# Scaling the first MLP's normalized tiles on ScalarE, and W1's splits put behind the first product

## The chip, the cores and the metric

The kernel runs on one core of a Trainium2 chip. A core has engines that each work through a queue of their own in order: TensorE (PE, with PEld for its weight loads), VectorE (DVE), ScalarE (ACT), GpSimd (POOL), and SyncE (SP), which issues most transfers. The metric is the device time of one execution in microseconds, lower is better.

## What is computed

The reference does three things in a row for 8 batches of 512 rows with 8 heads, and 32 state rows per batch. Attention runs both ways between the rows and the state. Its output, 4608 rows of 512 values, goes through a first MLP with a softmax gate and a normalization, and then through a second MLP with a sigmoid gate:

```python
# attention, both ways, concatenated to 4608 x 512
h = x @ w_in                                   # 512 -> 1024
sm = softmax(h)
solu = h * sm
mu = mean(solu); var = mean((solu - mu) ** 2)
ln = (solu - mu) / sqrt(var + 1e-06) * g_ln
x = ln @ w_out                                 # 1024 -> 512
h = x @ w_in2                                  # 512 -> 2048
out = (h * sigmoid(1.702 * h)) @ w_out2        # 2048 -> 512
```

Inputs are doubles; each is turned into 32-bit floats on the chip. A product with full accuracy is made of three matmuls: every factor is split into a high part, which is a cast, and a low part, which is a subtraction (`split` does this for weights, `mm3` is the three matmuls: high by high, high by low, low by high; in the profile lines 422, 423 and 424).

## The kernel before

The kernel doesn't issue instructions as it is written. Each step is recorded by `do(engines, function, reads, writes, key, after)`, with one or more engines that could do it and an assumed cost for each. `plan()` then puts the steps of all engines in an order, from the assumed costs and due times, chooses the engine where there is a choice, and gives each tile its buffer. `emit()` writes the instructions in that order. So a change of one step's engine, cost or predecessors shifts the choices for many other steps. `after=` names further steps that must be planned before this one; it stands for order only, no data goes between them.

The first MLP works on tiles of 128 rows: 4 tiles for each of the 8 batches, and 2 for the state rows, 34 in all. For one tile, `mlp1(b, i, key)` records:

- PE: the product that gives h (12 matmuls: two groups of heads, two halves of 512 columns, three each; 24 for the tiles of the state rows),
- DVE: the row maximum (L771); ACT: the exponential u, with its row sum (L773); DVE: u = h times u, with its row sum (L775),
- ACT: one value per row for the small term of the variance (L779); DVE: minus the mean into column 3 of the small tile `s` (L780),
- ACT: the sum of (u - mean) squared (L781); DVE: the variance into column 6 (L783),
- POOL: column 6 to the power -0.5 into column 7 (L785), one value per row,
- DVE or POOL: u = (u + column 3) * column 7 over 128x1024 values (L786), in place.

What follows reads u: `z_T` transposes four tiles' blocks of 128 columns on PE (L827), ACT makes the high part while it scales by g (L833), DVE the low part (L835), and `mlp1_out` multiplies by W2. From batch 3 to 7 one half of the columns goes through `z_turn` instead, which transposes on DVE (L797) and with transfers. The gated tile in PSUM takes a pair of banks; at most three such pairs are in use at once.

W1 is used in two ways. For batches 0 and 1 it is multiplied unsplit by the state rows' transposes (`state_w1`, L671). From batch 2 on, products with split W1 are used (`state_w1_both`), and the eight splits (4 blocks of rows by 2 halves of the columns; `hi_w1s` is a cast on ACT or DVE, `lo_w1s` a subtraction on POOL or DVE, L458) are recorded in the main loop with batch 1, before batch 1's attention. Their due times come from `W1S`; nothing else holds them back.

The second MLP (from about 420 us on) has its weights prepared earlier, between the batches.

## Time and profile before

| | us |
| --- | --- |
| median of 3 runs | 1127.77 (1125.75 to 1128.52) |
| profiled execution | 1126.07 |
| its span in the profile | 1124.3 |
| PE busy | 1080.0 (96%) |
| DVE busy | 825.2 (73%) |
| ACT busy | 637.8 (57%) |
| POOL busy | 258.7 (23%) |

The shares are averages over the whole span. To read what paces the kernel, one looks at busy times stretch by stretch, since the attention and first MLP (up to some 350 us) and the second MLP have different limits. Then the waits of PE name who released it, and the timeline shows what stood in that engine's queue. Mean durations hide that one and the same operation may take very different times when another engine works beside it; the timeline shows single ones.

### The profile page before, as it was taken

The page shows a single profiled execution, that of the slowest core. Times are in us where ns is not written, and L with a number is a line of the kernel's source. Part 1 is how long each engine was busy: PE and PEld are TensorE (multiplying, and loading weights), DVE is VectorE, ACT ScalarE, POOL GpSimd, SP SyncE. Part 2 cuts the span into 40 slices and gives each one's busy share as a digit, 9 for nine tenths or more (in the row PEclk, how much of TensorE's full clock was granted, in tenths as well). Part 3 has the DMA queues.
Part 4 walks back from the last instruction along what each step waited for, and adds up shares of the span by engine and source line. Part 5 has one row for each costly group of instructions (what it writes and reads, how often), then busy time and mean ns, then how long its engine had stood idle before and what let it go on. Part 6 is the DMA issues. An engine that isn't in the chain of part 4 may idle for free.

```text
span 1124.3 us, 21689 instructions
## 1 busy us (share of the span) xinstructions
PE 1080.0 (96%) x8055; PEld 976.9 (87%) x8055; DVE 825.2 (73%) x1398; ACT 637.8 (57%) x1171; POOL 258.7 (23%) x218
## 2 busy tenths in 40 slices
PE   6798999799899999999999999999999999999998
PEld 2466677577677889999999999999999999999998
DVE  6999878988989746628757755634388888788874
ACT  6686756866868546547666656545244444344341
POOL 3865443743746701301111000000000000000000
PEclk8899999999999999999999999999999999999999
DMA  8214234568673569998667657559944254344431
GB/s 242 67 39 113 78 70 135 165 126 177 187 162 87 158 153 365 334 374 276 230 233 242 237 204 257 179 209 398 383 145 125 64 170 150 101 144 151 134 93 57
DMA packets 233082, 202.78 MB, mean 180 GB/s; under 512 B 128784, under 2 KB 174864, under 8 KB 232976
## 3 DMA queue, kind: packets, MB, share of 16 engines
q1 hardware_dynamic: 232880, 201.26, 57.3%
q8 instruction: 63, 1.03, 0.4%
q14 instruction: 43, 0.35, 0.1%
q10 hardware_dynamic: 96, 0.13, 0.1%
HBM read 113.25 MB, written 82.84 MB: 174 GB/s over the span
## 4 chain that ended last, share of the span: by engine, by line
PE 75%; DVE 13%; issue 3%; SPq 3%; POOL 3%; DMA 2%; ACT 1%; DVEq 0%; POOLq 0%; ACTq 0%
PE psum L1098 9%; PE psum L1100 9%; PE psum L1099 9%; PE psum L1010 9%; PE psum L1011 9%; PE psum L1012 9%; PE psum L422 5%; PE psum L423 5%; PE psum L424 4%; DVE w_w L449 1%; DVE w_w L444 1%; SPq L529 1%; POOL lo_w3s L458 1%; DVE w_w L447 1%; DVE u L775 1%
## 5 line engine op out<-in xcount | busy, mean ns | idle before, releaser
L1098 PE MATMUL psum<-w4r,hi_g 128*128 128x256 f32 x896 | 251.8, 281 | 1.6 <-DVE oc L1109 1.6
L1100 PE MATMUL psum<-w4r,lo_g 128*128 128x256 f32 x896 | 251.6, 281 | 0.0
L1099 PE MATMUL psum<-w4r,hi_g 128*128 128x256 f32 x896 | 251.6, 281 | 0.0
L1098 PEld LDWEIGHTS psum<-w4r,hi_g 128*128 128x128 f32 x896 | 169.1, 189 | 1.8 <-ACT hi_g L463 1.8
L1100 PEld LDWEIGHTS psum<-w4r,lo_g 128*128 128x128 f32 x896 | 169.3, 189 | 0.0
L1099 PEld LDWEIGHTS psum<-w4r,hi_g 128*128 128x128 f32 x896 | 169.0, 189 | 0.0
L463 ACT CAST hi_g<-a_g 128x512 fp32r<-128x512 f32 x124 | 75.4, 620 | 127.3 <-DVE a_g L880 87.1
L451 POOL TENSOR_TENSOR w_w<-w_w,raw_w 128x512 uint32<-128x512 uint32 x48 | 68.9, 1441 | 284.1 <-DVE w_w L449 206.1
L1022 DVE TENSOR_TENSOR c<-psum,u 128x512 f32<-128x512 f32 x64 | 44.1, 689 | 98.0 <-PE psum L1012 63.7
L422 PE MATMUL psum<-zhi,hi_w 128*128 128x512 f32 (+1 forms) x288 | 113.9, 395 | 1.3 <-DVE zlo L835 0.6
L424 PE MATMUL psum<-zhi,lo_w 128*128 128x512 f32 (+1 forms) x288 | 109.9, 382 | 0.0
L957 DVE TENSOR_TENSOR lo_g<-a_g,hi_g 128x512 fp32r<-128x512 f32 x128 | 84.0, 685 | 19.9 <-PE psum L1099 7.1
L994 ACT ACTIVATE t<-c 128x512 f32<-128x512 f32 x96 | 60.5, 632 | 50.0 <-DVE c L1022 49.9
L957 DVE TENSOR_TENSOR lo_g<-gr,hi_g 128x512 fp32r<-128x512 f32 x104 | 71.0, 685 | 11.8 <-ACT hi_g L463 9.2
L423 PE MATMUL psum<-zlo,hi_w 128*128 128x512 f32 (+1 forms) x208 | 78.3, 376 | 0.2
L463 ACT CAST hi_g<-gr 128x512 fp32r<-128x512 f32 x104 | 61.8, 618 | 28.4 <-PE psum L1099 14.4
L422 PEld LDWEIGHTS psum<-zhi,hi_w 128*128 128x128 f32 x288 | 54.2, 188 | 17.3 <-issue 4.1
L424 PEld LDWEIGHTS psum<-zhi,lo_w 128*128 128x128 f32 x288 | 54.1, 188 | 11.8 <-DVE lo_w L458 0.4
L1010 PE MATMUL psum<-hi_x,w3r_1h 128*128 128x256 f32 x224 | 63.1, 282 | 1.2 <-ACT u L1017 1.2
L1011 PE MATMUL psum<-lo_x,w3r_2h 128*128 128x256 f32 x224 | 63.1, 282 | 0.0
L1010 PE MATMUL psum<-hi_x,w3r_2h 128*128 128x256 f32 x224 | 63.0, 281 | 0.0
L1011 PE MATMUL psum<-lo_x,w3r_3h 128*128 128x256 f32 x224 | 63.0, 281 | 0.0
(261 smaller groups left out, 3101.9 us busy)
## 6 DMA issues: line engine op xcount, KB each, us to landing
g<-t SPq DMA_DIRECT2D x136, 256.0 KB, 3.4
gr<-g SPq DMA_DIRECT2D x136, 256.0 KB, 3.4
w4r<-w4k SPq DMA_DIRECT2D x56, 256.0 KB, 5.2
raw_w<-in_moe_w_in SPq DMA_DIRECT2D x24, 512.0 KB, 6.0
raw_w<-in_moe_w_out SPq DMA_DIRECT2D x24, 512.0 KB, 4.2
xb<-scr SPq DMA_DIRECT2D x34, 256.0 KB, 6.3
scr<-x SPq DMA_DIRECT2D x16, 512.0 KB, 3.6
out<-oc SPq DMA_DIRECT2D x32, 256.0 KB, 3.8
```

What stands on the lines that cost most here:

```text
L422: nc.tensor.matmul(o, lhi, rhi, start=first, stop=False)
L423: nc.tensor.matmul(o, lhi, rlo, start=False, stop=False)
L424: nc.tensor.matmul(o, llo, rhi, start=False, stop=last)
L451: do(POOL(1.23), lambda e: e.tensor_tensor(u(), u(), raw()[:, :, 0], op=ALU.add), [w, raw], [w], key=due)
L463: e.copy(o, i)
L957: do(DVE(.68), lambda e: e.tensor_tensor(flat_(lo), flat_(t), flat_(hi), op=ALU.subtract), [t, hi], [lo], key=due)
L1010: nc.tensor.matmul(o, wh()[:, k, cut], hi()[:, k, :], start=first and not mi + k, stop=False, **OPEN)
L1011: nc.tensor.matmul(o, wh()[:, k, cut], lo()[:, k, :], start=False, stop=False, **OPEN)
L1012: nc.tensor.matmul(o, wl()[:, k, cut], hi()[:, k, :], start=False, stop=bool(mi and k), **OPEN)
L1098: nc.tensor.matmul(o, hi()[:, mi, cut], wt[:, 0], start=first, stop=False, **OPEN)
L1099: nc.tensor.matmul(o, hi()[:, mi, cut], wt[:, 1], start=False, stop=False, **OPEN)
L1100: nc.tensor.matmul(o, lo()[:, mi, cut], wt[:, 0], start=False, stop=2 * j + mi == NM - 1 and u == 1, **OPEN)
```

## The change

The scaling of the normalized tile is written as u = u * r + m * r with r the power -0.5 of the variance and m minus the mean, and is done by ACT in place of DVE or POOL. For that, POOL's step computes two columns: r in column 7 (as before; line 786 of the new kernel) and m * r in column 8 (line 787). Its assumed cost goes from .46 to .92; the ACT step (line 790) is assumed at 1.1. It applies to all 34 tiles.

`split` gets a parameter `after`, given to the cast. The eight W1 splits pass `after=[first0]`, where `first0` is the last product step of batch 0's first tile, `mlp1(0, 0)`. Everything else is as it was; lines after the first MLP are 3 higher, later ones up to 5.

```diff
@@ -451,10 +451,10 @@
         do(POOL(1.23), lambda e: e.tensor_tensor(u(), u(), raw()[:, :, 0], op=ALU.add), [w, raw], [w], key=due)
         return w
 
-    def split(w, name, due, shape=(512,), pair=None, low=(("pool", 1.23), ("dve", .6))):
+    def split(w, name, due, shape=(512,), pair=None, low=(("pool", 1.23), ("dve", .6)), after=()):
 
         hi, lo = pair or [tl("s", [P, *shape], F32R, f"{h}_{name}") for h in ("hi", "lo")]
-        do([("act", .52), ("dve", .335)], lambda e: copy(e, hi(), w()), [w], [hi])
+        do([("act", .52), ("dve", .335)], lambda e: copy(e, hi(), w()), [w], [hi], after=after)
         do(list(low), lambda e: e.tensor_tensor(lo(), w(), hi(), op=ALU.subtract), [w, hi], [lo], key=due)
         return hi, lo
 
@@ -782,9 +782,12 @@
            [u, s], [s])
         do(DVE(.13), lambda e: e.tensor_scalar(s()[:, 6:7], s()[:, 4:5], 1.0 / F1, s()[:, 5:6], op0=ALU.mult,
                                                op1=ALU.add), [s], [s])
-        do(POOL(.46), lambda e: e.tensor_tensor(s()[:, 7:8], s()[:, 6:7], half_p, op=ALU.pow), [s], [s])
-        do([("dve", .72), ("pool", 1.2)], lambda e: e.tensor_scalar(u(), u(), s()[:, 3:4], s()[:, 7:8], op0=ALU.add, op1=ALU.mult),
-           [s, u], [u])
+        def root(e):
+            e.tensor_tensor(s()[:, 7:8], s()[:, 6:7], half_p, op=ALU.pow)
+            e.tensor_tensor(s()[:, 8:9], s()[:, 3:4], s()[:, 7:8], op=ALU.mult)
+
+        do(POOL(.92), root, [s], [s])
+        do(ACT(1.1), lambda e: e.activation(u(), u(), AF.Identity, bias=s()[:, 8:9], scale=s()[:, 7:8]), [s, u], [u])
         return mm
 
     def z_turn(b, half, due):
@@ -1218,12 +1221,14 @@
         if b + 1 == DIRECT:
             for f in range(2):
                 for k in range(KD):
-                    W1s[k, f] = split(W1[k, f], f"w1s_{k}_{f}", b * SLOT + W1S + 2 * (k + KD * f))
+                    W1s[k, f] = split(W1[k, f], f"w1s_{k}_{f}", b * SLOT + W1S + 2 * (k + KD * f), after=[first0])
         if b + 1 < B:
             attention(b + 1)
         for i in range(C):
             step = SLOT / C if b < B - 1 else SLOT / 6
             last[b] = mlp1(b, i, b * SLOT + M1B + i * step if b else M1A + i * M1S)
+            if not b and not i:
+                first0 = last[0]
         if b == B - 1:
             key = b * SLOT + C * SLOT / 6
             for j in range(KD // 2):
```

What this does to the order shows at three places. First POOL's queue early in the kernel, up to about 50 us in the trace of before: `lo_w1s` are the low parts of W1, `alo` the low part of batch 0's and 1's attention, lines 596 and 603 steps of their softmax. Before:

```order
L458 TENSOR_TENSOR lo_w1s_0_536<-w_w_0_0_336,hi_w1s_0_479 128x512
L603 TENSOR_TENSOR s_0_1_393<-s_0_1_393,z_0_1_524 128x512
L451 TENSOR_TENSOR w_w_2_1_464<-w_w_2_1_464,raw_w_2_1_328 128x512
L451 TENSOR_TENSOR w_w_3_1_489<-w_w_3_1_489,raw_w_3_1_390 128x512
L610 TENSOR_TENSOR alo_1_584<-aT_1_565,ahi_1_571 128x512
L458 TENSOR_TENSOR lo_w1s_0_604<-w_w_1_0_360,hi_w1s_0_482 128x512
L596 TENSOR_TENSOR s_1_0_599<-s_1_0_599,m_1_0_606 128x512
L596 TENSOR_TENSOR s_1_1_612<-s_1_1_612,m_1_1_615 128x512
L458 TENSOR_TENSOR lo_w1s_0_639<-w_w_2_0_380,hi_w1s_0_554 128x512
L603 TENSOR_TENSOR s_1_0_599<-s_1_0_599,z_1_0_637 128x512
```

And after:

```order
L610 TENSOR_TENSOR alo_1_570<-aT_1_555,ahi_1_562 128x512
L596 TENSOR_TENSOR s_1_0_583<-s_1_0_583,m_1_0_588 128x512
L596 TENSOR_TENSOR s_1_1_592<-s_1_1_592,m_1_1_595 128x512
L603 TENSOR_TENSOR s_1_0_583<-s_1_0_583,z_1_0_617 128x512
L603 TENSOR_TENSOR s_1_1_592<-s_1_1_592,z_1_1_641 128x512
L610 TENSOR_TENSOR alo_0_708<-aT_0_679,ahi_0_702 128x512
L610 TENSOR_TENSOR alo_1_733<-aT_1_710,ahi_1_722 128x512
L458 TENSOR_TENSOR lo_w1s_0_779<-w_w_0_0_336,hi_w1s_0_775 128x512
L458 TENSOR_TENSOR lo_w1s_0_790<-w_w_1_0_360,hi_w1s_0_777 128x512
L786 TENSOR_TENSOR sml_0_670<-sml_0_670,half_p 128x1
```

The W1 subtractions that stood between the softmax steps are gone from there; the first two follow behind batch 1's attention (`alo`), the others later, among W2's.

Second, ACT's queue around batch 0's four squares (`junk` is their unused output; `u` and `sml` are the tile and its small columns; `zhi`, further down, is the high part of the transposed tile). Before:

```order
L675 CAST vhi_1_1_849<-psum 128x512
L463 COPY stT_851<-psum 128x256
L463 COPY xs_517<-psum 64x2x32
L781 ACTIVATE junk,sml_0_691<-u_0_705,sml_0_691 128x1024
L781 ACTIVATE junk,sml_1_717<-u_1_732,sml_1_717 128x1024
L781 ACTIVATE junk,sml_2_746<-u_2_761,sml_2_746 128x1024
L781 ACTIVATE junk,sml_3_803<-u_3_814,sml_3_803 128x1024
L773 ACTIVATE u_0_910,sml_0_897<-psum,sml_0_897 128x1024
L463 COPY xT_2_921<-psum 128x512
L463 COPY xT_3_924<-psum 128x512
L463 CAST sthi_934<-stT_851 128x2x2x64
L773 ACTIVATE u_1_937,sml_1_918<-psum,sml_1_918 128x1024
```

And after:

```order
L781 ACTIVATE junk,sml_0_670<-u_0_681,sml_0_670 128x1024
L675 CAST vhi_0_1_811<-psum 128x512
L779 ACTIVATE sml_3_773<-sml_3_773,eps 128x1
L675 CAST vhi_1_1_822<-psum 128x512
L781 ACTIVATE junk,sml_1_693<-u_1_706,sml_1_693 128x1024
L781 ACTIVATE junk,sml_2_720<-u_2_735,sml_2_720 128x1024
L781 ACTIVATE junk,sml_3_773<-u_3_788,sml_3_773 128x1024
L790 ACTIVATE u_0_681<-u_0_681,sml_0_670 128x1024
L790 ACTIVATE u_1_706<-u_1_706,sml_1_693 128x1024
L790 ACTIVATE u_2_735<-u_2_735,sml_2_720 128x1024
L790 ACTIVATE u_3_788<-u_3_788,sml_3_773 128x1024
L463 COPY xT_2_889<-psum 128x512
```

The four scalings (line 790) stand behind the four squares in ACT's queue. The first square has moved ahead of two casts of line 675, the copies `stT` and `xs` that stood ahead of the squares are gone to DVE, and batch 1's first exponential (line 773), which followed the squares, comes much later.

Third, PE's queue ahead of the first transposes of batch 0's normalized tiles. `vhi`, `vlo`, `ahi`, `alo` are the factors of batch 1's first MLP. Before, these were the last six matmuls of the third tile of batch 1, and then the transposes:

```order
L422 MATMUL psum<-vhi_1_0_823,ahi_1_750 128x512
L423 MATMUL psum<-vlo_1_0_837,ahi_1_750 128x512
L424 MATMUL psum<-vhi_1_0_823,alo_1_763 128x512
L422 MATMUL psum<-vhi_1_1_849,ahi_1_750 128x512
L423 MATMUL psum<-vlo_1_1_860,ahi_1_750 128x512
L424 MATMUL psum<-vhi_1_1_849,alo_1_763 128x512
L827 MATMUL psum<-ident,u_0_705 128x128
L827 MATMUL psum<-ident,u_1_732 128x128
L827 MATMUL psum<-ident,u_2_761 128x128
L827 MATMUL psum<-ident,u_3_814 128x128
```

And after, where they belong to batch 1's first tile:

```order
L423 MATMUL psum<-vlo_1_0_809,ahi_1_722 128x512
L424 MATMUL psum<-vhi_1_0_798,alo_1_733 128x512
L422 MATMUL psum<-vhi_1_1_822,ahi_1_722 128x512
L423 MATMUL psum<-vlo_1_1_833,ahi_1_722 128x512
L424 MATMUL psum<-vhi_1_1_822,alo_1_733 128x512
L830 MATMUL psum<-ident,u_0_681 128x128
L830 MATMUL psum<-ident,u_1_706 128x128
L830 MATMUL psum<-ident,u_2_735 128x128
L830 MATMUL psum<-ident,u_3_788 128x128
L830 MATMUL psum<-ident,u_0_681 128x128
```

Before, three tiles of batch 1 (36 matmuls), a product of scores and a state transpose stood ahead of the transposes since batch 1's first product began; now one tile (12 matmuls) does. The second tile follows behind two blocks of transposes, and the third and fourth after products with W2 have begun.

## Rows read from the trace of the kernel before

**Rows 1.** Busy us by stretch: PE, PEld, DVE, ACT, POOL, then PE clock, DMA.

```profile
40.00:62.00 22.00, 22.00 (x149) 13.44 (x149) 20.77 (x38) 17.06 (x35) 17.72 (x15) 0.92 0.00 1
62.00:78.00 16.00, 15.93 (x82) 11.17 (x80) 14.78 (x32) 13.74 (x30) 11.88 (x11) 1.00 0.07 24
78.00:107.00 29.00, 24.35 (x108) 17.54 (x108) 28.48 (x49) 20.60 (x38) 14.31 (x13) 1.00 0.52 134
107.00:128.00 21.00, 18.06 (x141) 12.84 (x141) 19.25 (x37) 18.36 (x33) 15.30 (x15) 1.00 0.36 102
...
183.00:224.00 41.00, 35.14 (x219) 25.97 (x219) 39.80 (x69) 30.57 (x56) 29.92 (x24) 1.00 0.49 141
...
280.00:316.00 36.00, 30.60 (x194) 22.53 (x193) 34.29 (x57) 30.38 (x56) 25.26 (x21) 1.00 0.64 180
...
420.00:1100.00 680.00, 677.16 (x5698) 675.33 (x5697) 467.24 (x759) 350.51 (x617) 37.99 (x25) 1.00 0.64 216
```

**Rows 2.** Waits of PE in 0 to 350 us: releaser, total us, times, longest.

```profile
PE psum L621 <- ACT e2t L583: 10.7, 4, 4.2
...
PE psum L827 <- POOL u L786: 2.4, 2, 1.5
```

**Rows 3.** Groups by line, 0 to 420 us: busy us, mean ns, idle before.

```profile
L781 ACT ACTIVATE junk<-u,sml 128x1024 bf16<-128x1024 f32 x34 | 39.0, 1147 | 14.2 <-DVE sml L780 13.9
...
L786 POOL TENSOR_SCALAR u<-u,sml 128x1024 f32<-128x1024 f32 x28 | 35.9, 1284 | 2.3
...
L785 POOL TENSOR_TENSOR sml<-sml,half_p 128x1 f32<-128x1 f32 x34 | 21.4, 632 | 53.3 <-DVE sml L783 53.2
...
L458 POOL TENSOR_TENSOR lo_w1s<-w_w,hi_w1s 128x512 fp32r<-128x512 f32 x8 | 10.5, 1323 | 0.0
...
L786 DVE TENSOR_SCALAR u<-u,sml 128x1024 f32<-128x1024 f32 x6 | 6.2, 1034 | 4.2 <-POOL sml L785 4.2
```

**Rows 4.** Timeline, 24 to 46 us: start, length, engine, line, operation, tiles.

```profile
26.12 0.75 DVE L447 TENSOR_SCALAR w_w<-w_w 128x512 uint32<-128x512 uint32 x2
...
32.48 1.48 POOL L458 TENSOR_TENSOR lo_w1s<-w_w,hi_w1s 128x512 fp32r<-128x512 f32 x1
...
32.74 1.84 DVE L447 TENSOR_SCALAR w_w<-w_w 128x512 uint32<-128x512 uint32 x2
...
39.97 2.02 PE L571 MATMUL psum<-xT,stT 128*64 128x512 f32 x4 [3.84 <-DVE vlo L676]
```

**Rows 5.** Timeline, 62 to 83 us, at batch 0's normalized tiles.

```profile
64.35 1.15 ACT L781 ACTIVATE junk<-u,sml 128x1024 bf16<-128x1024 f32 x1
...
67.02 0.40 PE L424 MATMUL psum<-vhi,alo 128*128 128x512 f32 x1
...
68.17 1.15 ACT L781 ACTIVATE junk<-u,sml 128x1024 bf16<-128x1024 f32 x1
...
72.24 2.38 POOL L786 TENSOR_SCALAR u<-u,sml 128x1024 f32<-128x1024 f32 x2
...
74.18 2.35 PE L827 MATMUL psum<-ident,u 128*128 128x128 f32 x16
```

**Rows 6.** Busy time and granted PE clock (0.62) just after the wait at 39.97.

```profile
40.00:44.50 4.50, 4.50 (x10) 2.19 (x10) 4.40 (x8) 3.32 (x7) 4.09 (x4) 0.62 0.00 0
```

**Rows 7.** Groups of DVE by line, 62 to 128 us.

```profile
L458 DVE TENSOR_TENSOR lo_w<-w_w,hi_w 128x512 fp32r<-128x512 f32 x2 | 2.5, 1274 | 0.0
...
L465 DVE CAST hi_v<-v 128x512 fp32r<-128x512 f32 x2 | 0.8, 398 | 0.0
...
L465 DVE COPY v<-psum 64x512 f32<-64x512 f32 x1 | 0.7, 672 | 0.0
```

**Rows 8.** Timeline, 78 to 108 us: one DVE operation twice, and POOL's addition.

```profile
81.11 0.41 DVE L444 TENSOR_SCALAR w_w<-w_w 128x512 f32<-128x512 f32 x1
...
82.95 1.31 POOL L451 TENSOR_TENSOR w_w<-w_w,raw_w 128x512 uint32<-128x512 uint32 x1 [3.12 <-ACT raw_w L445]
...
83.29 1.25 DVE L444 TENSOR_SCALAR w_w<-w_w 128x512 f32<-128x512 f32 x1
```

## The prediction

> **What bounds the kernel now.** I read the busy times by stretch first [rows 1]: each row gives the stretch, then the busy time of PE, PE's weight loads, DVE, ACT and POOL. From 420 us to 1100 us PE works 677.16 of 680 us, and the second MLP's long products fill it; the change touches nothing there, so that part has a fixed length and only its start can move. What can move it lies before: from 78 to 107 PE works 24.35 of 29 us while DVE works 28.48, from 107 to 128 it is 18.06 of 21 against DVE's 19.25, and in 183 to 224 and 280 to 316 PE lacks 5.86 and 5.40 us. In those stretches another engine paces PE. From 40 to 78 PE is full (22.00 of 22, 15.93 of 16). The waits of PE in the first 350 us [rows 2] name the engines: ScalarE's exponential for 10.7 us in four waits, and the step that the change moves, POOL's scaling of u, for 2.4 us in two. So the end follows this rule: what PE loses or gains in idle time before 350 us arrives at the end, and work on another engine counts only where that engine ends PE's wait.
>
> **The change, part by part.** The sum is made against the profiled execution, 1126.07 us (span 1124.3), which lies 1.70 below the median of 1127.77; I add the result to the median.
>
> The W1 splits. Eight casts on ACT and eight subtractions on POOL (1323 ns each [rows 3]) now come behind the first MLP's first product. The first subtraction ran at 32.48 for 1.48 us, beside two DVE operations on 512 columns that took 1.84 us; the same pair without a neighbour took 0.75 us [rows 4]. DVE then has no gap up to the tile that PE waits 3.84 us for, at 39.97. So taking this neighbour away gives 1.84 - 0.75 = 1.1 us on the path. **Term: -1.1 us.** The other seven stood in 40 to 62 where PE is full, so taking them from there gives nothing in that place. Where they go is in the stretch that DVE paces, which is counted below.
>
> The scaling. On POOL it took 1284 ns on average x28, on DVE 1034 ns x6 [rows 3]. ACT has no such operation in the trace; its nearest row is the square over the same 128x1024 values (1147 ns), with an accumulator read behind it that the new one lacks [rows 3]. I take 1.15 us: 34 x 1.15 = 39 us more on ACT; it could be a little less, since nothing is summed, and the range of the next terms covers that. POOL loses 35.9 us and gets 34 more operations on one column (632 ns each by the row of the power [rows 3], 21 us).
>
> Batch 0's four tiles. Now the four squares run on ACT from 64.35 to 68.17 + 1.15 = 69.3, and POOL's last pair of scalings ends at 72.24 + 2.38 = 74.62, just as PE, filled by three products of batch 1, reaches the transposes at 74.18 [rows 5]. In the new order only the first of these products stands ahead of the transposes, and the four squares and four scalings stand nearly in a row on ACT. PE would come there at 67.02 + 0.40 = 67.4, where that product ended [rows 5]. ACT would end the fourth scaling at 69.3 + 4 x 1.15 = 73.9 if it began as before; since copies ahead of the squares go to DVE and the first square is queued before two casts that waited for PE, I estimate 71. That is a new wait of PE for ACT of 3.6 to 6.5 us. It is not lost outright: the products that it postpones (about 9 us of matmuls) are then filling for 78 to 107, where PE idled 4.65 us, and the transposes come up to 3 us sooner than they did, so DVE's chain behind them starts sooner too. One more price: after the wait of 3.84 us PE's clock stood at 0.62 on average over the next 4.5 us [rows 6], between the levels of 1.2 and 2.4 GHz, which is 4.5 x 0.38 = 1.7 us. The most is 6.5 + 1.7 - 4.65 = 3.6; the least is zero, if all is refilled (3.6 against 4.65). **Term: +1, from 0 to +3.6**, near the low end because DVE, not PE, sets the end of this stretch.
>
> Who is full from 62 to 128. Adding the three rows [rows 1], DVE works 62.5 of 66 us and ACT 52.7. ACT gets eight scalings (8 x 1.15 = 9.2) and six W1 casts, for which I take half a square since they have half its columns (6 x 0.6 = 3.6), and gives copies to DVE that I put at 2.7: 62.8 of 66. DVE gets those copies (two of 512 columns at 0.67, two of half that size, and casts at 0.40 and less [rows 7], together 2.7), one W1 subtraction and one of W2 (0.7 to 1.3 each, about 2), and loses two subtractions of W2 at 1.27 [rows 7] and one scaling (1.03 to 1.7): about +1. Then five of POOL's W1 subtractions now fall beside DVE in this stretch. What a POOL neighbour costs DVE here is shown by one operation on 512 columns: alone 0.41 us, with POOL's addition beside it 1.25 us [rows 8]; the pair above lost 1.1. Not each neighbour meets such an operation; half of these prices is 0.4 to 0.55, five times that is 2.1 to 2.7. Against it stand the scalings that leave POOL at 107 to 128. Sum for DVE: +2 to +3 of work against 3.5 us of idle time. **Term: +2, from 0 to +5** (all five at 1.1 is 5.5; nothing if the idle time takes it).
>
> The later tiles. In 183 to 224 and 280 to 316 three and two or three scalings leave POOL, the POOL part of the 2.4 us of waits may go, and DVE is disturbed less; ACT rises by 1.15 each, from 30.57 and 30.38 to about 34 of 41 and 33.8 of 36 us [rows 1], and PE's waits there for ACT's exponential (10.7 us [rows 2]) lie behind the new work in ACT's queue. I see no row that decides it. **Term: 0, from -4** (the 2.4 and some three disturbances of 0.5) **to +4** (three or four scalings in front of an exponential that PE waits for). After 350 us PE is full and nothing counts.
>
> Sum: -1.1 + 1 + 2 + 0 = +1.9. Predicted: 1127.77 + 1.9 = **1129.7 us**.
>
> Two pages bear on it. The two rows with and without a POOL neighbour [rows 4, 8] show DVE stretched by about the length of POOL's operation. The Trainium skill, page "SBUF — State Buffer", section "Who interferes with whom", says that DVE and GpSimd share a port pair, held for a whole instruction, and that ScalarE waits for nobody; the trace agrees. By that rule alone each scaling that leaves POOL can free DVE for up to its length, and the time would fall as in the second rival below. The other speaks against the change: a scaling on DVE took 1.03 us and ACT's nearest row is above that [rows 3]. The Trainium skill, page "ScalarE: Activation LUTs", section "Rules for kernel authors", says to do additions and multiplications on VectorE and not on ScalarE. By it the eight scalings of this stretch would be 8 x 1.03 = 8.2 us on DVE, 70.7 of 66 us; the trace sets the fuller engine against the rule, so I do not follow it here.
>
> **The rivals.** *Slower: ACT's queue becomes the pace.* In ACT's single queue four scalings stand ahead of what PE and DVE need next (copies of x, W1 and W2 casts, the first gated tile). For it: 62.8 of 66 us in the estimate, 33.8 of 36 in 280 to 316, and that ACT's exponential is PE's largest wait already. Against it: PE has 9 us of postponed products. Price: the wait at 67 at its upper end (+3.6), the stretch to 128 at +3, one later exponential behind a scaling at +1, less 1.1: +6.5, or 1134.3 us. It decides from the point where PE's wait for the fourth scaling passes the 4.65 us that can be refilled.
>
> *Faster: DVE gets rid of its neighbour.* POOL's scalings at 62 to 78 and in the later stretches stop stretching DVE, and PE's waits for them go. Twelve of them lie in stretches that PE does not fill or just before one; 2.4 of waits, three to four disturbances of 0.5 that counted, and the W1 subtractions fall into DVE's gaps: -1.1 + 0 + 0 - 4 = -5.1, with 1 more if the earlier start of the transposes carries through: -6.1, or 1121.7 us. Against it: as many POOL operations enter the stretch that DVE paces as leave it.
>
> *The change doesn't do what it says* is not open: every engine runs its queue in the order that was laid down, and in it the splits do stand behind the first product.
>
> **How the numbers follow.** The forecast, between -3.4 and +3.4 us of the median, gets 0.40; the slower rival 0.38, since the new wait is certain and only its refilling is not; the faster one 0.22. A measurement of this kernel can tell about 0.3%, 3.4 us, from no change: so faster 0.22, same 0.40, slower 0.38. The range takes the faster rival's price at its lower side and nearly three us beyond the slower rival's, 1121.5 to 1137; all upper ends together (+11.5, 1139.3) are left out, as are all lower ends together with a neighbour price of 1.1.
>
> **What would show it.** The pair of DVE operations near 33 us at about 0.75 us, and PE's wait before 40 shorter by about 1.1 us: the first term. A wait of PE for ACT's scaling at about 67 us of 3.6 to 6.5 us, with a lower clock behind it, and less PE idle time in 78 to 107: the second. DVE near full from 62 to 128 with POOL's W1 subtractions beside stretched operations on 512 columns: the third. PE's waits for ACT's exponential unchanged in their sum (10.7 us): the fourth. The prediction is wrong on the slow side if PE is idle for more than 6 us at 67 and its idle time to 128 grows, and on the fast side if PE's idle time in 183 to 224 and 280 to 316 falls by several us while DVE's operations on 512 columns there get shorter.

## The result: 0.62% slower

The changed kernel takes 1134.99 us (median of 6 runs, 1133.78 to 1136.47), the kernel before 1127.80 beside it; the ratio is 1.0062 with a 95% interval of 1.0044 to 1.0081. That is 7.2 us more. The profiled execution took 1134.99 us, its span is 1133.2 (before 1124.3), so the two traces differ by 8.9 us.

Two sums of the page say what these 8.9 us are made of. PE's matmuls are the same 8055, but PE was busy for 1084.8 us in place of 1080.0: 4.8 us more, at a mean granted clock of 0.986 in place of 0.992. The rest, 8.9 - 4.8 = 4.1 us, is more idle time of PE. So about half of the two traces' difference is waiting, and half is work done at a lower clock. This is a count of where the time stands, not yet a cause, and over all runs the clock's part is smaller: 0.992 is high for the kernel before. The 50 runs of it that stand beside the experiments below have a median clock of 0.989, the six of the changed kernel 0.9855. At one and the same clock of 0.986 the kernel before took 1127.0 to 1132.5 us (six runs, median 1129.1) and the changed kernel 1133.8 and 1135.0 us (two runs), so some 5 us remain without it.

The busy times by stretch of the changed kernel (columns as in [rows 1]):

```profile
40.00:62.00 22.00, 20.98 (x160) 13.19 (x158) 20.58 (x43) 18.07 (x36) 9.33 (x9) 1.00 0.00 1
62.00:78.00 16.00, 11.26 (x41) 8.56 (x41) 14.96 (x30) 15.57 (x26) 10.47 (x14) 0.79 0.21 67
78.00:107.00 29.00, 24.28 (x112) 17.50 (x113) 28.22 (x45) 20.18 (x38) 19.36 (x15) 1.00 0.34 91
107.00:128.00 21.00, 18.70 (x134) 14.31 (x133) 18.53 (x38) 19.39 (x32) 11.42 (x15) 0.92 0.45 102
...
183.00:224.00 41.00, 39.11 (x240) 28.95 (x240) 37.80 (x70) 35.25 (x64) 20.00 (x21) 1.00 0.37 93
...
280.00:316.00 36.00, 31.59 (x190) 22.54 (x189) 35.53 (x66) 28.98 (x56) 20.88 (x18) 0.95 0.66 180
...
420.00:1100.00 680.00, 676.90 (x5663) 673.13 (x5662) 464.82 (x752) 350.09 (x618) 36.69 (x25) 1.00 0.65 219
```

Against [rows 1]: from 62 to 78 PE falls from 15.93 to 11.26 us; from 78 to 107 it works no more than before (24.28 against 24.35 us) although the postponed products were there to be done; 183 to 224 is better (39.11 against 35.14), 280 to 316 has about the same busy time (31.59 against 30.60), but at a granted clock of 0.95. From 420 us on nothing differs but the start. ACT has gone from 52.7 to 55.1 us in 62 to 128, and its own idle time there is small only up to 78 (15.57 of 16 us).

PE's waits in the first 350 us (releaser, total us, times, longest), against [rows 2]:

```profile
PE psum L621 <- ACT e2t L583: 6.2, 2, 3.5
...
PE psum L422 <- DVE xT L465: 4.7, 1, 4.7
...
PE psum L422 <- ACT v L463: 2.2, 1, 2.2
...
PE psum L830 <- ACT x L463: 1.1, 1, 1.1
```

The waits for POOL's scaling are gone. The exponential of line 583 is the attention's; only its two waits before 20 us are left (6.2 us). Before, 7.3 of its 10.7 us lay there too, and 3.4 at 246 and 291 us. New are 4.7 us for a copy `xT` on DVE, 2.2 for the copy `v` and 1.1 for the copy `x` on ACT. Summed from 60 to 350 us, PE waits 19.0 us for DVE where it waited 14.0 before, 3.9 for ACT where it waited 4.0, and 0.5 for POOL where it waited 2.4. So it is DVE that PE waits longer for, not ACT.

The four stretches in which the trace of the changed kernel has the clock at 0.5 after 55 us, at the lower of its two levels of 1.2 and 2.4 GHz (columns as in [rows 1], the clock is the third number from the end):

```profile
66.50:73.30 6.80, 6.00 (x16) 4.74 (x17) 6.00 (x10) 6.80 (x11) 5.44 (x6) 0.50 0.49 157
124.50:128.00 3.50, 3.47 (x8) 2.79 (x9) 1.24 (x2) 2.99 (x4) 0.48 (x1) 0.51 0.56 190
227.00:233.80 6.80, 6.03 (x16) 4.84 (x17) 6.77 (x13) 5.29 (x11) 2.82 (x3) 0.50 1.01 375
312.30:315.70 3.40, 3.30 (x8) 2.38 (x9) 3.40 (x8) 3.35 (x8) 2.49 (x5) 0.50 0.66 128
```

PE was busy for 18.8 us in them, so 9.4 us of full-speed work were lost. The trace before has none after 45 us; it has more of it earlier (its mean granted clock up to 40 us is 0.83, that of the changed kernel 0.87). Each of the four begins at or just before the end of a wait of PE or a row of them: 4.66 us up to 67.30, 2.17 up to 124.53, 1.15 and 1.59 up to 227.77, 2.59 up to 312.25.

To see where the loss arises although the order differs, I give each matmul a fixed price by its columns, from rows at full clock (512 columns 0.233 us, 256 0.1175, 128 0.133 as a transpose, 64 0.04), and ask at what time a kernel has done as much as the kernel before had at time T. The difference is its lag, in us. (The first 20 us differ by -1.4 to +0.6 between executions, before any change acts.) The columns belong to the kernels of the experiments below. "New plan" is the changed kernel with one assumed cost altered, "order, POOL" the changed kernel's order with the scaling issued to POOL, "copies, two products" the kernel with four copies forward. The dummy matmuls count as no work.

| T | changed | new plan | order, POOL | ACT only | held, ACT | held, 8 tiles | copies sooner | copies, two products | copies, dummies |
| --- | --- | --- | --- | --- | --- | --- | --- | --- | --- |
| 30 | -1.1 | -0.6 | -1.0 | 0.0 | 0.6 | -0.5 | -0.5 | -0.9 | -0.6 |
| 40 | -2.2 | -1.6 | -2.0 | 0.0 | 0.6 | -0.5 | -1.6 | -2.0 | -1.7 |
| 60 | -2.8 | -1.6 | -2.5 | 0.5 | 1.0 | 0.5 | -1.6 | -1.1 | -1.7 |
| 75 | 5.5 | 5.7 | 8.3 | 8.1 | 5.7 | 5.4 | 7.3 | 8.4 | 7.1 |
| 130 | 4.3 | 1.7 | 4.6 | 1.4 | 9.5 | 9.4 | 6.2 | 7.7 | 4.8 |
| 190 | 3.8 | 1.1 | 4.2 | 0.8 | 9.5 | 9.4 | 5.7 | 7.2 | 4.4 |
| 220 | 0.6 | -2.2 | 1.6 | -2.5 | 9.0 | 10.4 | 2.4 | 3.9 | 1.1 |
| 240 | 4.8 | 1.4 | 6.7 | 1.0 | 9.3 | 9.4 | 4.7 | 7.2 | 3.5 |
| 300 | 3.5 | 0.4 | 5.3 | -0.2 | 13.5 | 10.6 | 4.2 | 5.9 | 3.1 |
| 320 | 8.2 | 9.0 | 12.7 | 5.2 | 13.5 | 11.6 | 8.9 | 10.6 | 7.8 |
| 440 | 9.5 | 11.0 | 15.9 | 7.3 | 16.4 | 12.2 | 11.6 | 13.5 | 8.4 |

The changed kernel gains 1.7 us from 30 to 60, loses 8.3 near 67, gets 1.2 back up to 130, gains 3.2 up to 220, loses 4.2 at 225 to 240 and 4.7 at 300 to 320, and 1.3 at the end of the first MLP, where a wait of 0.99 us for ACT's scaling stands at 366.26.

### The profile page after: what moved, and what is told of

It is laid out like the page before. It is cut to its first block, busy times and chain, and to the rows that moved or that the text cites. A ratio compares the mean times of both kernels' runs of the same rounds, so it can differ in the third digit from the quotient of the medians.

```text
span 1133.2 us, 21695 instructions
## 1 busy us (share of the span) xinstructions
PE 1084.8 (96%) x8055; PEld 982.2 (87%) x8055; DVE 827.1 (73%) x1405; ACT 670.8 (59%) x1195; POOL 226.8 (20%) x221
## 4 chain that ended last, share of the span: by engine, by line
PE 78%; DVE 13%; ACT 2%; issue 2%; SPq 2%; DMA 2%; POOL 0%; DVEq 0%; POOLq 0%; ACTq 0%
PE psum L1101 9%; PE psum L1102 9%; PE psum L1103 9%; PE psum L1013 9%; PE psum L1014 9%; PE psum L1015 9%; PE psum L422 6%; PE psum L423 5%; PE psum L424 5%; DVE w_w L449 1%; DVE w_w L444 1%; PE psum L830 1%; DVE u L775 1%; SPq L809 1%; DVE sml L771 1%
## 5 line engine op out<-in xcount | busy, mean ns | idle before, releaser
L422 PEld LDWEIGHTS psum<-zhi,hi_w 128*128 128x128 f32 x288 | 55.4, 192 | 15.9 <-issue 3.2
L424 PEld LDWEIGHTS psum<-zhi,lo_w 128*128 128x128 f32 x288 | 55.1, 191 | 11.5
```

Of the source, the lines that this page charges most:

```text
L422: nc.tensor.matmul(o, lhi, rhi, start=first, stop=False)
L424: nc.tensor.matmul(o, llo, rhi, start=False, stop=last)
```

## The experiments

Two theories stood first. *Engine*: the scaling in ACT's queue costs by itself. *Order*: any new plan leaves the order that suited the hardware, and that costs, whichever engine scales. The ratios below are to runs of the kernel before on the same chip.

**The parts alone.** ACT scales, and the splits don't wait (one line, against the changed kernel):

```diff
-W1s[k, f] = split(W1[k, f], f"w1s_{k}_{f}", b * SLOT + W1S + 2 * (k + KD * f), after=[first0])
+W1s[k, f] = split(W1[k, f], f"w1s_{k}_{f}", b * SLOT + W1S + 2 * (k + KD * f))
```

> The scaling is done by ACT as in the changed kernel; W1's splits do not wait. Two theories. Engine theory: the 7.2 us come from the scaling standing in ACT's queue (PE waits and a halved clock after them), and the W1 part gave about 1 us back; then this kernel takes 1135 to 1137 us with an early loss near 62 to 73 us of 5 us or more. Order theory: the planner, given other costs, lays out another order than the one that its numbers were tuned for, and that order costs; then this kernel can land anywhere between 1127 and 1140 us, and the places of its losses differ from those of the changed kernel.

Measured: 1131.71 us against 1126.73, ratio 1.0038 (1.0024 to 1.0052). And the splits' wait alone, with the scaling as before (against the kernel before; the parameter and the call, as in the change, are left out):

```diff
-do([("act", .52), ("dve", .335)], lambda e: copy(e, hi(), w()), [w], [hi])
+do([("act", .52), ("dve", .335)], lambda e: copy(e, hi(), w()), [w], [hi], after=after)
...
```

> W1's splits wait for the first product; the scaling stays on DVE and POOL. Engine theory: about 1 us faster than before, 1126 to 1128 us, since only a neighbour of DVE is moved. Order theory: several us slower, 1130 to 1138 us, because the order behind it is a new one. The first term of the prediction holds under both if the pair of DVE operations near 32 us falls from 1.84 to about 0.75 us.

Measured: 1125.88 us, ratio 0.9991 (0.9975 to 1.0007): no difference that can be told. The pair of operations of line 447 took 0.75 us there and in the changed kernel (start us, length, engine, line; below, the changed kernel against [rows 4]), and PE's wait before 38 us is 0.8 us shorter than that of [rows 4] in the changed kernel. With the splits' wait alone it is 3.77 us, hardly shorter, but the lag (worked out as in the table above) falls there too, from -0.8 to -1.9 between 30 and 40 us:

```profile
25.04 0.75 DVE L447 TENSOR_SCALAR w_w<-w_w 128x512 uint32<-128x512 uint32 x2
...
31.65 0.75 DVE L447 TENSOR_SCALAR w_w<-w_w 128x512 uint32<-128x512 uint32 x2
...
37.80 1.63 PE L571 MATMUL psum<-xT,stT 128*64 128x512 f32 x4 [3.01 <-DVE vlo L676]
```

The loss thus belongs to the ACT part. Together the parts lose 0.62%, alone 0.38% and -0.09%; the intervals of 0.62% and 0.38% overlap, but the profiles differ at one place. These are ACT alone from 62 to 128 us:

```profile
62.00:78.00 16.00, 11.15 (x48) 7.69 (x45) 14.22 (x35) 14.80 (x24) 7.81 (x12) 0.79 0.22 67
78.00:107.00 29.00, 28.66 (x134) 21.03 (x133) 28.21 (x51) 21.01 (x41) 15.30 (x13) 1.00 0.34 91
107.00:128.00 21.00, 18.81 (x141) 13.68 (x139) 16.22 (x30) 19.73 (x34) 11.54 (x15) 1.00 0.45 101
```

It regains its early loss, PE working 28.66 of 29 us in 78 to 107, where the changed kernel has 24.28. There POOL works 15.30 us, in the changed kernel 19.36, with three W1 subtractions more (five in 62 to 128). DVE's eight operations of line 447 on W2 in 62 to 128 show the neighbour (busy us, mean ns). ACT only:

```profile
L447 DVE TENSOR_SCALAR w_w<-w_w 128x512 uint32<-128x512 uint32 x8 | 4.1, 515 | 0.2
```

And the changed kernel:

```profile
L447 DVE TENSOR_SCALAR w_w<-w_w 128x512 uint32<-128x512 uint32 x8 | 7.3, 909 | 0.2
```

That is 3.2 us more on the engine that paces the stretch. Against it speaks that with the splits waiting but the scaling as before, the same eight took 8.3 us and nothing was lost. The new plan of the changed kernel, below, speaks against it too: POOL works 20.25 us in 78 to 107 there, and yet 4.0 us of the lag come back from 75 to 130. So this cost may explain why the changed kernel regains only 1.2 us, but that is not shown.

**New plans with nothing else changed.** One assumed number of the planner each: the cost of the scaling on POOL in the kernel before, and that of POOL's two small operations in the changed one.

```diff
-do([("dve", .72), ("pool", 1.2)], lambda e: e.tensor_scalar(u(), u(), s()[:, 3:4], s()[:, 7:8], op0=ALU.add, op1=ALU.mult),
+do([("dve", .72), ("pool", 1.28)], lambda e: e.tensor_scalar(u(), u(), s()[:, 3:4], s()[:, 7:8], op0=ALU.add, op1=ALU.mult),
```

> The kernel before with a single assumed number changed: the planner's cost of the scaling on POOL is 1.28 in place of 1.2. Every step does the same work; only the order and some choices of engine are planned anew. Engine theory: no difference, 1126.5 to 1129 us. Order theory: a loss of the size of the change's own, 1131 to 1138 us, from waits in new places.

```diff
-do(POOL(.92), root, [s], [s])
+do(POOL(.85), root, [s], [s])
```

> The changed kernel with a single assumed number changed: the planner's cost of POOL's two small operations is 0.85 in place of 0.92. Engine theory: no difference to the changed kernel, 1133.5 to 1136.5 us. Order theory: another time, anywhere from 1127 to 1140 us, more than 2 us away from 1135.

Measured: 1124.97 us, ratio 0.9985 (0.9975 to 0.9995), and 1136.19 us, ratio 1.0085 (1.0070 to 1.0100). A new plan of the kernel before is no slower; it is 1.8 us faster than that kernel, and the fastest one here; a new plan of the changed kernel is as slow as it. In these two cases the order theory fails as far as the time goes: re-planning moves it by some 2 us, not by 7. The places move, though. The new plan of the changed kernel regains most of its early loss (a lag of 5.7 us at 75, 1.7 at 130, -2.2 at 220) and then loses 8.6 us from 300 to 320 where the changed kernel loses 4.7. So the early loss alone does not set the end.

**The order held, the engine swapped.** A step gets a field for the engine that it is issued to, and the plan is made as if nothing had changed; the order of PE's queue is then the same to the matmul. The cut shows the field's use and the scaling; POOL's step also computes the second column, and the splits don't wait.

```diff
-                s.fn(engines[s.on])
+                s.fn(engines[s.force or s.on])
...
-        do([("dve", .72), ("pool", 1.2)], lambda e: e.tensor_scalar(u(), u(), s()[:, 3:4], s()[:, 7:8], op0=ALU.add, op1=ALU.mult),
+        t = do([("dve", .72), ("pool", 1.2)], lambda e: e.activation(u(), u(), AF.Identity, bias=s()[:, 8:9], scale=s()[:, 7:8]),
+        t.force = "act"
```

> The order of before is kept to the step (planned with the old costs), but where the scaling stood in that order it is now issued to ACT, and POOL computes the two columns. W1's splits do not wait. Engine theory: the scaling in ACT's queue costs by itself, 1131 to 1136 us. Order theory: no loss, 1124 to 1129 us, perhaps a gain of 1 to 3 us where PE waited 2.4 us for POOL's scaling.

Measured: 1139.92 us against 1128.95, ratio 1.0108 (1.0081 to 1.0136). More than the engine theory asked for. PE's waits up to 350 us name ACT (releaser, total us, times, longest):

```profile
PE psum L621 <- ACT e2t L583: 12.7, 4, 5.4
...
PE psum L555 <- ACT xT L463: 2.7, 1, 2.7
...
PE psum L422 <- ACT v L463: 1.8, 2, 1.6
PE psum L832 <- ACT v L463: 1.4, 1, 1.4
PE psum L832 <- ACT u L790: 1.4, 2, 1.2
```

Of the exponential's 12.7 us, 8.1 lie before 20 us, ahead of any scaling. From 60 to 350 us PE waits 13.4 us for ACT; in the kernel before it was 4.0, with 2.4 for POOL. It isn't mainly the scaled tile that PE waits for (1.4 us), nor the exponential (4.5, before 3.4), but the copies in ACT's queue (7.5, before 0.6). The scalings hold these up in two ways, by their own 42.0 us and by what ACT waits ahead of them (the whole kernel):

```profile
L790 ACT ACTIVATE u<-u,sml 128x1024 f32<-128x1024 f32 x34 | 42.0, 1239 | 20.3 <-POOL sml L787 20.2
```

For 20.2 us ACT stands idle until POOL has the second column; in the changed kernel it is 9.0. In this order the scaling comes right behind POOL's step, which suited POOL's own scaling. So the kernel shows what ACT's queue costs in an order that was made for another engine, not what it costs in the changed kernel.

The other way round, the order of the changed kernel with the scaling issued to POOL (POOL's step computes one column again, not shown here):

```diff
-do(ACT(1.1), lambda e: e.activation(u(), u(), AF.Identity, bias=s()[:, 8:9], scale=s()[:, 7:8]), [s, u], [u])
+t = do(ACT(1.1), lambda e: e.tensor_scalar(u(), u(), s()[:, 3:4], s()[:, 7:8], op0=ALU.add, op1=ALU.mult), [s, u], [u])
+t.force = "pool"
```

> The order of the changed kernel is kept to the step, but the scaling is issued to POOL as one operation, as most were before. Engine theory: the 7.2 us come back, 1126 to 1130 us. Order theory: the loss stays or grows, 1134 to 1140 us, because PE still waits near 62.6 for a copy in DVE's queue and the fill in PE's queue is unchanged.

Measured: 1142.65 us, ratio 1.0131 (1.0109 to 1.0153). Here the engine theory misses. Most waits of the changed kernel are there (5.20 us near 68 for the same copy, 2.59 for `sr` near 314), with waits for POOL's scaling added (0.95 and 2.52 us). An order made for one engine doesn't suit the other, in either direction.

This kernel also tells where the changed kernel's two later losses come from. In the table the changed kernel loses 4.2 us from 220 to 240 and 4.7 from 300 to 320; its order with POOL's scaling loses 5.1 and 7.4 there, at the same waits (PE alone). The changed kernel:

```profile
225.09 1.09 PE L830 MATMUL psum<-ident,u 128*128 128x128 f32 x8 [1.15 <-ACT x L463]
227.77 1.11 PE L830 MATMUL psum<-ident,u 128*128 128x128 f32 x4 [1.59 <-DVE zlo L838]
...
312.25 0.69 PE L648 MATMUL psum<-ident,sr 128*128 128x128 f32 x2 [2.59 <-DVE sr L641]
```

And its order with POOL's scaling:

```profile
227.01 1.09 PE L827 MATMUL psum<-ident,u 128*128 128x128 f32 x8 [2.00 <-ACT x L463]
229.69 1.12 PE L827 MATMUL psum<-ident,u 128*128 128x128 f32 x4 [1.59 <-DVE zlo L835]
...
314.10 0.69 PE L648 MATMUL psum<-ident,sr 128*128 128x128 f32 x2 [2.59 <-DVE sr L641]
```

ACT alone and the new plan lose in both stretches too. The order of before with all scalings on ACT loses nothing to speak of in either (0.3 and 0.0), though 4.2 us between them. So, as far as single traces tell, these two losses come with the orders that were planned for ACT's scaling, and not from ACT's time for it.

**Which tiles.** The order of before is held; in the first kernel ACT scales only the eight tiles of batches 0 and 1, in the second only the two that PE had waited for.

```diff
+        on_act = b <= 1
```

> The order of before, held; ACT does the scaling for the eight tiles of batches 0 and 1 alone, the other 26 stay on DVE and POOL. The held kernel with all 34 on ACT lost 11 us. Queue theory (a scaling costs where ACT's queue is full and PE is next behind it, which is from 62 to 131 us): these eight carry more than half, 1132 to 1137 us, with the waits near 75 and 130 us as there. Even theory (each scaling costs about the same, 11/34 us): 8 x 0.32 = 2.6 us, 1129.5 to 1131.5 us.

```diff
+        on_act = (b, i) in ((1, 2), (3, 3))
```

> The order of before, held; ACT does the scaling for two tiles alone, the third of batch 1 and the last of batch 3, which are the ones that PE waited 0.92 us (and 0.22 us for its neighbour on DVE) and 1.46 us for. Queue theory: ACT had idle time ahead of both, so these waits shrink and nothing else moves: 0.5 to 2.5 us faster, 1125 to 1127.5 us. Even theory: 0.6 us slower, 1128 to 1129 us.

Measured: 1136.95 us against 1126.27, ratio 1.0077 (1.0044 to 1.0110), for the eight; 1129.18 us, ratio 1.0026 (1.0009 to 1.0043), for the two. So eight tiles of 34 carry 0.77 of the 1.08% (two intervals that overlap), and the even theory (2.6 us) falls. The table of lags shows it: up to 130 us the kernel with eight and that with all 34 are the same, +9.4 and +9.5 us. This is how the first step of it comes about in the kernel with eight (start us, length, engine, line):

```profile
71.56 1.23 ACT L794 ACTIVATE u<-u,sml 128x1024 f32<-128x1024 f32 x1
...
72.70 1.09 ACT L773 ACTIVATE u<-psum,sml 128x1024 f32<-128x1024 f32 x1
...
73.79 0.57 ACT L463 COPY xT<-psum 128x512 f32<-128x512 f32 x1
...
74.41 0.44 PE L555 MATMUL psum<-ident,S 128*128 128x128 f32 x2 [2.69 <-ACT xT L463]
```

A scaling and then an exponential run on ACT, and only behind both comes the copy `xT`, which PE waits 2.69 us for at 74.41. (Another scaling ran at 68.01, after 0.64 us of waiting for POOL.) Two more such waits, for `v`, follow at 129 and 131 us, and the clock is halved after both places.

The two tiles did not gain what I expected. PE's waits there became 1.56 us (for a copy `v` behind the scaling on ACT) and 1.18 us, in place of 0.92 with 0.22, and 1.46. Their kernel's lag is 0.4 us at 280 us; the 3 us that follow arise where its profile has the clock halved after waits of 2.98 and 2.10 us near 292 and 316, waits that are in the kernel before too (2.29 and 1.72) without a halved clock. Whether that is the two tiles' doing stays open.

**The wait at 67 us.** The trace of the changed kernel at this place (start us, length, engine, line; against [rows 5]):

```profile
61.11 1.15 ACT L781 ACTIVATE junk<-u,sml 128x1024 bf16<-128x1024 f32 x1
...
64.80 4.62 ACT L790 ACTIVATE u<-u,sml 128x1024 f32<-128x1024 f32 x4
...
66.55 0.69 DVE L465 COPY xT<-psum 128x512 f32<-128x512 f32 x1
...
67.30 0.80 PE L422 MATMUL psum<-vhi,ahi 128*128 128x512 f32 x1 [4.66 <-DVE xT L465]
...
72.58 1.41 PE L830 MATMUL psum<-ident,u 128*128 128x128 f32 x8
```

The prediction had PE come to the transposes at 67.4 and wait for ACT's fourth scaling, which was estimated to end at 71. The scalings end earlier, at 64.80 + 4.62 = 69.4, but PE doesn't get that far: from 62.64 it waits 4.66 us to begin batch 1's first product, whose bank still holds the transposes of batch 2's `xT`. Their copy has moved from ACT to DVE, where it stands at 66.55 behind W2's preparation and behind the small step that waits for ACT's fourth square. In the first experiment on this, three copies go ahead of W2's preparation in DVE's queue; in the second, batch 1's second product also goes ahead of the transposes in PE's.

```diff
+    pl.sooner([pl.find("dve", n, True) for n in ("xT2_0", "stT2", "xT2_1")], pl.find("dve", "w_w2_0"))
```

> The changed kernel; three copies of batch 2 (two xT, one stT) are moved forward in DVE's queue, ahead of the preparation of W2's first block, so that PE's bank for batch 1's first product is free sooner. Theory A (the wait of 4.66 us at 62.64 for that copy is the cause at this place): the wait goes, the clock does not fall, and 5 to 8 us of the lag at 70 us come back, of which 2 to 5 us reach the end: 1130 to 1133 us. Theory B (the wait for ACT's scalings, as the prediction had it, stands right behind): batch 1's first product runs at about 62.6 to 65.5, and PE then waits some 4 us for the fourth scaling that ends at 69.4; the end changes by less than 1.5 us, 1133.5 to 1136 us.

```diff
+    pl.sooner([pl.find("dve", n, True) for n in ("xT2_0", "stT2", "xT2_1")], pl.find("dve", "w_w2_0"))
+    pl.sooner([s for s in pl.order if s.on == "pe" and any(t.name == "h1_1" for t in s.tiles)], pl.find("pe", "pz0_0"))
```

> As the kernel with the copies moved forward, and besides the second product of batch 1 is put ahead of the first transposes in PE's queue, so that PE has about 2.8 us more to do before it needs ACT's scalings. Theory A: little more than the copies alone, within 1 us of it. Theory B: PE's wait near 66 falls to 1 to 1.5 us, the clock stays up, and the time falls by 2 to 5 us against the changed kernel, 1130 to 1133 us.

Measured: 1135.81 us, ratio 1.0066 (1.0041 to 1.0092), and 1137.60 us, 1.0086 (1.0064 to 1.0109), both against 1128.95. The copies alone give theory B. The product now begins at 64.44, and PE waits for one scaling after the other (PE alone):

```profile
67.34 0.28 PE L844 MATMUL psum<-ident,u 128*128 128x128 f32 x1
68.41 0.33 PE L844 MATMUL psum<-ident,u 128*128 128x128 f32 x1 [0.80 <-ACT u L804]
69.55 0.33 PE L844 MATMUL psum<-ident,u 128*128 128x128 f32 x1 [0.80 <-ACT u L804]
70.68 1.58 PE L844 MATMUL psum<-ident,u 128*128 128x128 f32 x5 [0.80 <-ACT u L804]
```

Four scalings pace four transposes, 1.07 to 1.14 us apart, and nothing is gained. The second kernel did not fill the wait: its product was held for 5.79 us by the bank of a fourth copy, `stT`. So that copy goes forward too; and in another kernel, with the three copies, 13 matmuls on a constant tile run ahead of the first transposes, so that PE is busy while ACT scales.

```diff
-("xT2_0", "stT2", "xT2_1")
+("xT2_0", "stT2", "xT2_1", "stT3")
```

> As the kernel with copies moved forward and the second product of batch 1 ahead of the transposes, with a fourth copy (the second stT, for which that product waited 5.79 us there) moved forward too. If PE's wait for ACT's scalings and the halved clock behind it are what costs near 67 us: PE is busy to 70 us, the clock stays at full, the lag at 75 us falls from 7 to 9 us to under 2 us, and the end comes 3 to 6 us sooner than the changed kernel, 1129 to 1132 us. If the gain of an early place is lost again behind it, since other engines pace the stretch to 128 us: the lag at 75 us falls but the time stays at 1133 to 1136 us.

```diff
         def go(e):
+            for _ in range(13 if not b and not k else 0):
+                e.matmul(p(), warm[:, 0:P], warm, start=True, stop=True)
             for i in range(n_tiles[b]):
```

> As the kernel with copies moved forward, with 13 matmuls on a constant tile put ahead of the first transposes of batch 0, into the same bank, so that PE is busy while ACT scales; they add nothing to the output. It measures the clock's part of the loss alone. With copies moved forward the clock was halved from 69.8 us for 6.8 us. If that halved stretch costs: it is gone, the lag at 80 us falls by 3 to 3.5 us, and the end comes 1 to 3.5 us sooner than with the copies alone, 1132 to 1134.5 us. If PE is paced by others behind it anyway: under 1 us at the end, 1135 to 1136.5 us.

Measured: 1135.98 us, ratio 1.0080 (1.0056 to 1.0104), and 1135.18 us, ratio 1.0077 (1.0053 to 1.0101), both against 1126.27. Neither gains. With two products ahead PE runs on, but then it waits at the next place, for DVE's low part of the gated tile (PE alone):

```profile
78.16 1.12 PE L844 MATMUL psum<-ident,u 128*128 128x128 f32 x4 [5.80 <-DVE zlo L852]
```

The lag at 75 us is 8.4, no better. With the dummies the halved stretch shrank from 6.8 to 3.4 us and the lag at 80 us hardly changed, from 6.8 to 6.7, and did not fall by 3 to 3.5; that trace ends 3.2 us sooner than the one with the copies alone, but the medians' intervals don't tell the two apart. So the early wait is not a single gate to be opened: each time PE is given something to do there, it waits further on for the next piece of the chain (squares, scalings, transposes, casts and copies) from ACT or DVE, 5.80 us here and 1.48 us for `stT` at 73.17 with the dummies.

## Why the prediction missed its likeliest case

The forecast was 1129.7 us, no change that can be told from none; the measured 1134.99 lies in the range of 1121.5 to 1137, near the slower rival's 1134.3, which had 0.38 against 0.40. The terms, one by one:

- **W1's first subtraction, -1.1 us.** Right. The pair at 31.65 took 0.75 us, and from 30 to 40 us the lag fell by 1.1. It fell by 1.0 to 1.1 in every kernel with the splits' wait, and in none without it.
- **The scaling on ACT.** Its rows (busy us, mean ns), against [rows 3]:

```profile
L790 ACT ACTIVATE u<-u,sml 128x1024 f32<-128x1024 f32 x34 | 41.5, 1238 | 9.3 <-POOL sml L787 9.0
...
L786 POOL TENSOR_TENSOR sml<-sml,half_p 128x1 f32<-128x1 f32 x34 | 22.1, 649 | 56.4 <-DVE sml L783 56.3
...
L458 POOL TENSOR_TENSOR lo_w1s<-w_w,hi_w1s 128x512 fp32r<-128x512 f32 x7 | 9.3, 1341 | 1.2 <-ACT hi_w1s L463 1.2
L787 POOL TENSOR_TENSOR sml<-sml 128x1 f32<-128x1 f32 x34 | 8.9, 262 | 2.7
```

  1238 ns, where I took 1.15 us from the square; one of the row of four at 64.80 costs 4.62 / 4 = 1.16 us. The Trainium skill, page "ScalarE: Activation LUTs", section "What ACT_TABLE_LOAD costs", gives for an activation 186 ns plus 0.833 ns an element and about 93 ns for each operand that is a column, and says that those in a row overlap by 93 ns: an estimate of 186 + 853 + 186 = 1225 ns, and 1132 in a row. The trace agrees within 25 ns. POOL's multiplication on one column took 262 ns, not the power's 632. None of this decided anything.
- **PE's new wait near 67 us, +1 (0 to +3.6).** This is a step that failed. The wait was there in its size (4.66 us, and 3.6 to 6.5 had been given), the lower clock behind it as well, but the refilling was not: the lag went up by 8.3 us at 67 and only 1.2 of that came back up to 130, where I had let 4.65 us be refilled. From 78 to 107 PE worked no more than before. The term should have stood at its upper end or over it. The sign that I had set for the slow side, more than 6 us of waiting at 67, was too high as well: 4.66 us were enough. That PE's idle time there could be refilled was not wrong in itself: ACT alone took back 6.7 us from 75 to 130, the new plan 4.0. Why this order did not stays open. The postponed work was also put too high: I had about 9 us, and the rows of before from 67.25 to 74.18 hold 6.9. The mechanism was half wrong too: the wait that ended last was for a copy that the change had moved to DVE, and the wait for the scalings stood behind it, as the kernel with the copies moved forward shows. I had noticed that copies move but asked only what they cost, not which bank of PE's they hold.
- **From 62 to 128, +2 (0 to +5).** The neighbours' price is seen on DVE (line 447 took 3.2 us more than with ACT alone), but what it did to the time is not shown. The two terms together, +6.6 at most as the slower rival took them, are what the lag shows from 60 to 130: -2.8 to 4.3, 7.1 us.
- **The later tiles, 0 (-4 to +4).** This term failed as well: from 130 to 440 us the lag rose by 5.2, just beyond the bound. 183 to 220 gained 3.2 us, as the faster rival had it, and the waits for POOL went; 225 to 240 and 300 to 320 lost 8.9, in both cases at a wait followed by a halved clock. What I had named as the danger did not come. I read the 10.7 us of [rows 2] as waits in these stretches, but 7.3 of them lie before 20 us, and the 3.4 that do lie there went away, so the sum did not stay at 10.7 as the fourth sign said. The two losses come with the order, as the changed kernel's order with POOL's scaling shows, and I had no term for a new order in these stretches. How much of them is the waits and how much the clock behind them was not separated.

Of the rivals, the slower one came close in the number, in part by luck. Its mechanism, ACT's queue, is seen near 67, where the scalings stand behind the copy's wait, and in the order of before held, which loses 11 us while PE waits for ACT, most of it with eight tiles. In the changed kernel itself PE waits no longer for ACT than before from 60 to 350 us (3.9 against 4.0 us), and the later exponential that the rival priced at +1 did not come; 8.9 us that it had no price for did, and 3.2 came back. How much of the 7.2 us is ACT's queue stays open. With ACT alone the planner's own order costs 0.38%, where the order of before costs 1.08%. The faster rival's cause was real, POOL's waits went, but small. The Trainium skill's rule that DVE and GpSimd, in the operations that it names, block each other ("SBUF — State Buffer", "Who interferes with whom") cut both ways, as the third term had it: POOL's busy time fell from 15.30 to 11.42 us in 107 to 128, but rose from 14.31 to 19.36 in 78 to 107, where W1's subtractions entered.

## What to carry to other kernels

An operation moved to an engine with idle time can cost what stands behind it in that engine's queue, and what the engine waits for ahead of it (20.2 us in the order of before), so look at what PE waits for next there, not at the engine's share of busy time. Idle time of PE in a stretch that other engines pace is no sure room to make up for a loss ahead of it: 1.2, 4.0 and 6.7 us came back in three plans of the same work. Ask of a sum of waits where they lie: 7.3 of the 10.7 us for the exponential lay ahead of everything that the change touched. Where a planner lays out the order, a new order can lose time far behind the place that was changed. And when a plan moves copies out of PSUM to another engine, ask which bank they free and who waits for that bank, before counting their microseconds.

## What the runs showed of the hardware

PE's granted clock fell after waits. After waits of about 2 to 5 us, or shorter ones close together (1.15 and 1.59 us near 226; 0.61, 0.80 and 0.80 up to 69.55 with the copies moved forward), it stood at the lower level for 3.4 or 6.8 us. But the same wait need not bring it: the one of 2.59 us near 312 was followed by a halved stretch of 3.4 us in the changed kernel's trace and by none in the trace with the copies moved forward, and the one of 2.51 us near 91 to 93 the other way round. Executions of one kernel differ along with it: among the 50 runs of the kernel before, the ten with a granted clock of 0.992 took 1124.5 to 1126.5 us, the six with 0.986 took 1127.0 to 1132.5. So differences of some 2 to 3 us between single traces are not read here as effects.
